# Top-32 attention: eight segments per head in place of nine, ScalarE shifts every column, the selection's product moved between two exchanges

## The chip, the core and the metric

The kernel runs on one core of a Trainium2 chip. The metric is the device time of one execution in microseconds (us). Names of engines: PE is TensorE (PEld its weight loads), DVE is VectorE, ACT is ScalarE, POOL is GpSimd, SP is SyncE, which issues most DMAs.

## What is computed

Attention over 2 batches of 8 heads, 576 tokens of 64 columns, where each query keeps only its 32 highest scores; its output goes to a layer of eight experts, of which each token takes one.

```python
scores = scale * np.matmul(q, k.transpose(0, 1, 3, 2))            # (2, 8, 576, 576)
kth = np.partition(scores, -top_k, axis=-1)[..., -top_k:-top_k + 1]   # top_k = 32
scores = np.where(scores >= kth, scores, -1000000000.0)
attn = np.exp(scores - np.max(scores, axis=-1, keepdims=True))
attn = attn / (np.sum(attn, axis=-1, keepdims=True) + 1e-09)
x = np.matmul(attn, v)                  # reshaped to (1152, 512)
logits = x @ w_gate                     # eight experts; argmax and softmax weight
h = np.maximum(x_e @ w1[e], 0.0)        # per expert e, at most 288 tokens
out = gate_w * (h @ w2[e])
```

The inputs are drawn from a normal distribution. Of each row of 576 scores the 32nd largest is needed exactly.

## The kernel before

**Tiling.** 1152 tokens are 9 tiles of 128, and 8 heads are 4 pairs, so there are 36 units u (`NU`), each 128 queries by two heads (j = 0, 1) by 576 scores. `scores(u)` lets PE write them into PSUM: `s0` (1024 wide, two banks) holds all 576 of head 0 and the first 64 (`TAIL`) of head 1, `s1` holds the other 512 of head 1. Both tiles exist once, so unit u+1 can be written only when all readers of unit u are through.

**The selection of a unit, on DVE.** `heads(u)` runs MAX8 (the eight largest of a row) over segments of each head's row: nine segments of 64 columns, 18 MAX8 (L312). A reduction takes each head's maximum (L315). The first list `nn` holds, negated, the first four or five of each segment (45 columns per head, some of them fillers from `keep`, L316); what is left of each segment's eight is the second list. `merge(u)` takes the eight smallest of the first list (`ns`, L325), removes them by an exchange (MATCH_REPLACE into `wk`, L336, one per head), takes the next eight (`na`, L340) and the eight largest of the second list (`vb`, L339). `bound(u)` makes a lower bound of the 32nd score out of `na` and `vb` (three small instructions, L347, L349, L351).

**The rest of a unit.** ACT's `shift(u)` (L356) reads the scores from PSUM and writes `sm` = maximum minus score into SBUF: 576 columns of head 0, then 512 of head 1; `shift_rest(u)` (L359) does the remaining 64 on DVE. ACT's `sign(u)` (L369) compares `sm` with the bound and counts; POOL's `turn(u)` (L376, two instructions) multiplies `sm` by the signs into `z`; DVE's `select(u)` finds by two MAX8 over 576 columns (L400, steps 1 and 2), a product (`ds`, L402, step 3) and a sum (`nk`, L404, step 4) the exact 32nd score out of the count's excess of 0 to 7. ACT's `penalty` (L413) and PE's and ACT's `probs` (transposes L432 and L433, exponential L434) and PE's `values` (L454, L457) end the unit. Where a count lies outside the range that eight places can mend, `check` sets a flag, and a plain second pass behind the experts computes everything again.

**Order.** The code is a software pipeline written out by hand: step i works on `heads(i)`, `sign`/`turn(i-1)`, `select(i-2)`, `probs(i-3)`, `values(i-4)`, and the scores of i+1. In step i DVE does, in this order, `heads(i)`, `select(i-2)` step 1, the `ns` of `merge(i)`, `shift_rest(i)`, `select(i-2)` step 2, and the rest of `merge(i)`. PE does `values(i-4)`, half of it ahead of `scores(i+1)` and half behind.

**Gaps.** Between two MAX8 of a head `heads` calls `fill()`, which issues one row of a list of small instructions: 8 gaps per head, 16 in a step. The list of a step starts with `bound` (3) and `select` step 0 (L397), then rows of `pick` and `pick_row` in a few steps (they choose the order of experts, from a count that PE's `tally`, L962, has made), three places for `normalise` (L468, L470, L473), and the route of a tile of tokens to its expert (L540 to L563). What does not fit into the gaps runs behind L316.

**Other work beside it.** From step 18 on POOL splits expert weights (L620, L622) in each step's rest; from step 31 on PE also computes the first expert's hidden layer (L661). The experts follow the last unit.

```python
picks = at(2, select, 1) + at(0, merge, None, 0) + at(0, shift_rest) + at(2, select, 2)
run(at(4, values, 0) + picks + at(-1, scores) + at(4, values, 1) + routes((1, 1.5, 3)) + routes((0, 3.5)))
small += at(2, select, 3) + at(2, select, 4)
run(at(0, merge, fill, 1))
```

Here `run(at(0, merge, fill, 1))` issues the rest of `merge`, and the two `fill()` in it issue `select` steps 3 and 4.

Of the kernel before, what the change touches and what calls it, by code (L numbers as in the profile page):

```python
# [19 lines left out]
FT = mybir.dt.float32  # L20
# [5 lines left out]
OP = mybir.AluOpType  # L26
# [3 lines left out]
SEG = 9  # L30
FOUR = 6
# [4 lines left out]
def kernel(  # L36
# [132 lines left out]
    UN = [consts.tile([128, 2, SEG, 9], FT, name=f"un{i}") for i in range(2)]  # L169
    keep = pd[:, 448:448 + 5 * SEG].rearrange("p (s c) -> p s c", s=SEG)  # L170
    nc.vector.memset(keep, -LOW)
    nc.vector.memset(keep[:, :FOUR, 0:1], LOW)
    for un in UN:
        nc.gpsimd.memset(un[:, :, :FOUR, 0:1], LOW)
        nc.gpsimd.memset(un[:, :, FOUR:, 8:9], LOW)
    VB = [pd[:, 32 * i:32 * i + 16].rearrange("p (j c) -> p j c", j=2) for i in range(2)]
# [120 lines left out]
    def segment(u, j, i):  # L297
        w = S // SEG
        if j == 0:
            return PS[u][0][:, i * w:i * w + w]  # L300
        return PS[u][1][:, (i - 1) * w:i * w] if i else PS[u][0][:, S:S + w]


    def heads(u, fill):
        un = UN[u % 2]
# [3 lines left out]
        for j in range(2):  # L309
            for i in range(SEG):  # L310
                o = int(i < FOUR)
                nc.vector.max(out=un[:, j, i, o:o + 8], in_=segment(u, j, i))  # L312
                if i < SEG - 1:
                    fill()
        nc.vector.tensor_reduce(out=mx[:, 0], in_=un[:, :, :, 0:2], axis=mybir.AxisListType.XY, op=OP.max)  # L315
        nc.vector.scalar_tensor_tensor(nn, un[:, :, :, 0:5], -1.0, keep[:, None].to_broadcast([128, 2, SEG, 5]),  # L316
                                       op0=OP.mult, op1=OP.min)
        VAL[u] = [mx, un, nn.rearrange("p j s c -> p j (s c)")]

    def merge(u, fill, half=None):  # L320
# [16 lines left out]
        fill()  # L337
        for j in range(2):
            nc.vector.max(out=vb[:, j], in_=un[:, j, :, 5:])  # L339
# [4 lines left out]
    def bound(u, step):  # L344
        mx, na, vb, tm = VAL[u]
        if step == 0:
            nc.vector.scalar_tensor_tensor(tm, na, -1.0, vb, op0=OP.mult, op1=OP.min)  # L347
# [6 lines left out]
    def shift(u):  # L354
        for j, (o, i) in enumerate(((SM[u][:, 0], PS[u][0][:, :S]), (SM[u][:, 1, TAIL:], PS[u][1]))):
            nc.scalar.activation(o, i, AF.Identity, bias=VAL[u][0][:, 0, j:j + 1], scale=-1.0)  # L356

    def shift_rest(u):
        nc.vector.tensor_scalar(SM[u][:, 1, :TAIL], PS[u][0][:, S:S + TAIL], -1.0, VAL[u][0][:, 0, 1:2],  # L359
                                op0=OP.mult, op1=OP.add)  # L360
# [1036 lines left out]
```

## Time and profile before

| what | us |
|---|---|
| three runs, median (lowest, highest) | 380.05 (379.45, 380.07) |
| the profiled execution, its own time | 379.64 |
| its span in the trace | 377.8 |
| steps 0 to 2 (from the reduction of step 0 to that of step 3) | 14.47 to 33.49 |
| steps 3 to 30 | 33.49 to 209.91 |
| steps 31 to 34 | 209.91 to 241.50 |
| rest of the last unit, routing, count of the experts' tokens | 241.50 to 288 |
| experts | 288 to 377.8 |

"Step i" in times means the stretch from the start of L315 for unit i to its start for unit i+1. A timeline row gives an instruction's start and its length; since instructions on one engine overlap at their ends, what an instruction costs its engine is the distance from its start to the next one's start, called pitch below. The idle time in brackets at the end of a row is the engine's wait before it and what ended the wait.

### The profile page before, as it was taken

How to read it: one execution, taken by the hardware profiler on the slowest of the kernel's cores; microseconds unless marked ns; L12 is line 12 of the kernel's file. 1: busy time of each engine (PE TensorE's matmuls, PEld its weight loads, DVE VectorE, ACT ScalarE, POOL GpSimd, SP SyncE). 2: the span in 40 equal slices, each digit the busy share in tenths (PEclk: the TensorE clock that was granted, in tenths of full speed). 3: DMA queues.
4: the chain of work that ended last, by engine and by line, in shares of the span. 5: the costliest groups of instructions: out<-in, count | busy, mean ns of one | idle time of the engine just before them, and what ended most of it. 6: DMA issues, size and time to landing. Idle time of an engine off the chain costs nothing. (4 is left out here: it accounts for less than half of the span.)

```text
span 377.8 us, 9896 instructions
## 1 busy us (share of the span) xinstructions
PE 318.9 (84%) x3383; PEld 264.7 (70%) x3383; DVE 321.4 (85%) x1708; ACT 278.5 (74%) x464; POOL 240.0 (64%) x280
## 2 busy tenths in 40 slices
PE   5676887798797888987878798999889999999990
PEld 3453666686676766776667687889635999997680
DVE  4879999999999999999999998777665769799930
ACT  5787988888888889898898597774336847786710
POOL 3976969598895598998988886994310101219321
PEclk9778999999999999999999899999999999999997
DMA  9529997948283920000301900832949999999100
GB/s 164 135 57 202 221 208 202 210 120 125 45 272 95 363 75 3 30 2 30 112 2 47 324 22 30 245 120 78 371 97 307 394 304 302 411 302 251 56 24 23
DMA packets 69922, 60.25 MB, mean 159 GB/s; under 512 B 52069, under 2 KB 52069, under 8 KB 69863
## 3 DMA queue, kind: packets, MB, share of 16 engines
q1 hardware_dynamic: 67719, 54.79, 52.9%
q0 software_dynamic: 1616, 4.73, 3.7%
q8 instruction: 28, 0.46, 0.5%
q14 instruction: 31, 0.25, 0.2%
q10 hardware_dynamic: 528, 0.02, 0.1%
HBM read 40.66 MB, written 12.09 MB: 140 GB/s over the span
## 5 line engine op out<-in xcount | busy, mean ns | idle before, releaser
L312 DVE MAX8 un<-s 128x8 f32<-128x64 f32 x648 | 107.0, 217 | 1.0 <-PE s L294 1.0
L376 POOL TENSOR_TENSOR z<-sm,sg 128x576 f32<-128x576 f32 x71 | 90.0, 1286 | 17.7 <-ACT sg L369 17.4
L457 PEld LDWEIGHTS pV<-vm,pT 128*128 128x128 f32 (+1 forms) x640 | 72.3, 183 | 6.9 <-issue 3.6
L681 POOL DMA_INDIRECT out_dram<-y,xp x12 | 24.4, 2032 | 79.8 <-DVE y L857 40.2
L457 PE MATMUL pV<-vm,pT 128*128 128x65 f32 (+1 forms) x640 | 73.2, 262 | 0.0
L413 ACT ACTIVATE pen<-sm,nk 128x576 bf16<-128x576 f32 x71 | 51.4, 768 | 20.6 <-DVE nk L404 20.5
L622 DVE TENSOR_TENSOR ws<-wr,ws 128x1024 bf16<-128x1024 f32 x52 | 61.9, 1238 | 3.3 <-ACT ws L616 2.9
L294 PE MATMUL s<-qk 128*128 128x512 f16 (+3 forms) x320 | 44.0, 297 | 16.8 <-DVE sm L359 16.8
L432 PE MATMUL p<-ident,sm 128*128 128x128 f32 x252 | 50.0, 286 | 7.3 <-ACT xT L526 7.2
L369 ACT ACTIVATE sg<-sm,mx 128x576 bf16<-128x576 f32 x72 | 54.8, 762 | 1.3 <-DVE mx L351 1.3
L400 DVE MAX8 z<-z 128x8 f32<-128x576 f32 x72 | 54.0, 752 | 1.3 <-POOL z L376 1.3
L356 ACT ACTIVATE sm<-s,mx 128x576 f32<-128x576 f32 x72 | 47.5, 711 | 9.7 <-DVE mx L315 9.0
L616 ACT ACTIVATE ws<-wr 128x2048 f16<-128x2048 f32 (+1 forms) x26 | 47.6, 1842 | 6.8 <-issue 4.4
L433 PE MATMUL p<-identB,pen 128*128 128x128 bf16 x252 | 46.0, 223 | 7.7 <-ACT pen L413 7.7
L661 PEld LDWEIGHTS <-ws 128*128 128x128 f16 (+1 forms) x768 | 49.0, 98 | 0.9 <-issue 0.4
L432 PEld LDWEIGHTS p<-ident,sm 128*128 128x128 f32 x252 | 37.0, 147 | 12.0 <-ACT xT L526 8.6
L433 PEld LDWEIGHTS <-pen 128*128 128x128 bf16 x324 | 33.9, 106 | 11.7 <-ACT pen L413 10.8
L294 PEld LDWEIGHTS <-qk 128*128 128x128 f16 (+1 forms) x320 | 20.2, 107 | 28.8 <-issue 20.8
L434 ACT ACTIVATE pT<-p 128x1152 f32<-128x1152 f32 x28 | 31.7, 1132 | 0.0
L622 POOL TENSOR_TENSOR ws<-wr,ws 128x1024 bf16<-128x1024 f32 x12 | 25.6, 2133 | 0.0
L454 PE MATMUL pV<-vt,pT 128*128 128x130 f32 (+1 forms) x80 | 18.1, 308 | 6.1 <-DVE r L540 2.9
L563 POOL DMA_INDIRECT xbuf<-xs,ru x9 | 10.5, 1166 | 17.2 <-DVE un L312 8.1
(277 smaller groups left out, 646.0 us busy)
## 6 DMA issues: line engine op xcount, KB each, us to landing
wr<-in_moe_w_dram SPq DMA_DIRECT2D x32, 1024.0 KB, 8.0
xbuf<-zero SPq DMA_DIRECT2D x6, 771.0 KB, 5.7
qnat<-in_q_dram SPq DMA_DIRECT2D x16, 144.0 KB, 3.4
knat<-in_k_dram SPq DMA_DIRECT2D x16, 144.0 KB, 3.7
out_dram<-zero SPq DMA_DIRECT2D x3, 768.0 KB, 4.7
vm<-in_v_dram SPq DMA_DIRECT2D x16, 128.0 KB, 3.1
qk<-qk SPq DMA_DIRECT2D x14, 144.0 KB, 2.4
vt<-in_v_dram SPq DMA_DIRECT2D x4, 64.0 KB, 4.6
```

The lines of the kernel that those rows point to most:

```text
L294: nc.tensor.matmul(PS[u][a][row:row + n, o:o + w], QK[b][2 * i][:, h, s:s + n], QK[b][1][:, h, c:c + w], start=(i == 0), stop=(i == 1))
L312: nc.vector.max(out=un[:, j, i, o:o + 8], in_=segment(u, j, i))
L369: nc.scalar.activation(SG[u][j], SM[u][:, j], AF.Sign, bias=VAL[u][0][:, 2, j:j + 1], scale=-(1.0 - 2.0 ** -20), accum_out=CNT[:, c:c + 1])
L376: engs[j].tensor_tensor(out=Z[u][:, j], in0=SM[u][:, j], in1=SG[u][j], op=OP.mult)
L400: nc.vector.max(out=z8[:, step - 1], in_=Z[u][:, step - 1])
L413: eng.activation(o, x, AF.Relu, bias=n)
L432: nc.tensor.matmul(pt[:, i], sm[:, cs], ident, start=True, stop=False, is_transpose=True)
L433: nc.tensor.matmul(pt[:, i], pen[:, cs], identB, start=False, stop=True)
L457: nc.tensor.matmul(PV[t][row:row + n, h0 + half], PT[u][:, 5 * half + c, row:row + n], VM[b][:, c, p, half], start=False, stop=(half == 1 ...
L616: nc.scalar.activation(w[:, 0, s], r[:, s], AF.Copy)
L622: eng.tensor_tensor(out=w[:, 1].bitcast(BF)[:, s], in0=r[:, s], in1=w[:, 0, s], op=OP.subtract)
L661: nc.tensor.matmul(o, a(i), c(i), start=(i == 0 and m == 0), stop=(i == k - 1 and m == 2))
```

## The change

- Eight segments per head: 8 of 72 columns for head 0; for head 1 the 64 columns in `s0` and seven pieces of `s1` (six of 73, one of 74). 16 MAX8 per unit over the same 1152 columns.
- The first list takes five of each of eight segments, 40 columns and no fillers; the second list has three of each, 24. `nn` becomes a plain product with a column of -1; `un` comes from the rotating pool `att`; `vb` gets a ninth column in front, which is infinite.
- `shift_rest` is gone; ACT's `shift` has three instructions: 576 columns, 64 columns, 512 columns.
- `select` step 2 is issued right behind step 1, ahead of `ns`; the first `fill()` in the second part of `merge`, which issues `select` step 3 (the product `ds`), moves from behind the two exchanges to between them.

```diff
--- before.py
+++ after.py
@@ -27,8 +27,7 @@
 BIG = float(2.0 ** 90)
 LOW = -3.0e38
 TOPK = 32
-SEG = 9
-FOUR = 6
+SEG = 8
 SPLIT = 256.0
 
 
@@ -166,14 +165,11 @@
 
 
     pd = psum.tile([128, 512], FT, name="pD", bufs=1)
-    UN = [consts.tile([128, 2, SEG, 9], FT, name=f"un{i}") for i in range(2)]
-    keep = pd[:, 448:448 + 5 * SEG].rearrange("p (s c) -> p s c", s=SEG)
-    nc.vector.memset(keep, -LOW)
-    nc.vector.memset(keep[:, :FOUR, 0:1], LOW)
-    for un in UN:
-        nc.gpsimd.memset(un[:, :, :FOUR, 0:1], LOW)
-        nc.gpsimd.memset(un[:, :, FOUR:, 8:9], LOW)
-    VB = [pd[:, 32 * i:32 * i + 16].rearrange("p (j c) -> p j c", j=2) for i in range(2)]
+    minus = pd[:, 448:449]
+    nc.vector.memset(minus, -1.0)
+    VB = [pd[:, 32 * i:32 * i + 18].rearrange("p (j c) -> p j c", j=2) for i in range(2)]
+    for vb in VB:
+        nc.vector.memset(vb[:, :, 0:1], -LOW)
     DM = [pd[:, 64 + 16 * i:80 + 16 * i].rearrange("p (j c) -> p j c", j=2) for i in range(2)]
     M1 = [pd[:, 96 + 2 * i:98 + 2 * i] for i in range(2)]
     tab = pd[:, 104:112]
@@ -295,26 +291,26 @@
                                      QK[b][1][:, h, c:c + w], start=(i == 0), stop=(i == 1))
 
     def segment(u, j, i):
-        w = S // SEG
         if j == 0:
+            w = S // SEG
             return PS[u][0][:, i * w:i * w + w]
-        return PS[u][1][:, (i - 1) * w:i * w] if i else PS[u][0][:, S:S + w]
+        w = 512 // (SEG - 1)
+        return PS[u][1][:, (i - 1) * w:i * w if i < SEG - 1 else 512] if i else PS[u][0][:, S:S + TAIL]
 
 
     def heads(u, fill):
-        un = UN[u % 2]
+        un = att([128, 2, SEG, 8], FT, name="un")
         nn = att([128, 2, SEG, 5], FT, name="nn")
         SM[u] = att([128, 2, S], FT, name="sm", tag="sm", bufs=4)
         mx = att([128, 4, 2], FT, name="mx4", bufs=3)
         for j in range(2):
             for i in range(SEG):
-                o = int(i < FOUR)
-                nc.vector.max(out=un[:, j, i, o:o + 8], in_=segment(u, j, i))
+                nc.vector.max(out=un[:, j, i], in_=segment(u, j, i))
                 if i < SEG - 1:
                     fill()
-        nc.vector.tensor_reduce(out=mx[:, 0], in_=un[:, :, :, 0:2], axis=mybir.AxisListType.XY, op=OP.max)
-        nc.vector.scalar_tensor_tensor(nn, un[:, :, :, 0:5], -1.0, keep[:, None].to_broadcast([128, 2, SEG, 5]),
-                                       op0=OP.mult, op1=OP.min)
+        nc.vector.tensor_reduce(out=mx[:, 0], in_=un[:, :, :, 0], axis=mybir.AxisListType.X, op=OP.max)
+        nc.vector.tensor_tensor(out=nn.rearrange("p j s c -> p (j s) c"), in0=un[:, :, :, 0:5].rearrange("p j s c -> p (j s) c"),
+                                in1=minus[:, None, :].to_broadcast([128, 2 * SEG, 5]), op=OP.mult)
         VAL[u] = [mx, un, nn.rearrange("p j s c -> p j (s c)")]
 
     def merge(u, fill, half=None):
@@ -334,9 +330,10 @@
         vb = VB[u % 2]
         for j in range(2):
             nc.vector.match_replace(out=wk[:, j], in_to_replace=ns[:, j], in_values=nn[:, j], imm_value=LOW)
-        fill()
+            if j == 0:
+                fill()
         for j in range(2):
-            nc.vector.max(out=vb[:, j], in_=un[:, j, :, 5:])
+            nc.vector.max(out=vb[:, j, 1:9], in_=un[:, j, :, 5:])
             nc.vector.max(out=na[:, j], in_=wk[:, j])
         fill()
         VAL[u] = [mx, na, vb, tm]
@@ -344,7 +341,7 @@
     def bound(u, step):
         mx, na, vb, tm = VAL[u]
         if step == 0:
-            nc.vector.scalar_tensor_tensor(tm, na, -1.0, vb, op0=OP.mult, op1=OP.min)
+            nc.vector.scalar_tensor_tensor(tm, na, -1.0, vb[:, :, 0:8], op0=OP.mult, op1=OP.min)
         elif step == 1:
             nc.vector.tensor_reduce(out=M1[u % 2], in_=tm, axis=mybir.AxisListType.X, op=OP.max)
         else:
@@ -352,12 +349,9 @@
 
 
     def shift(u):
-        for j, (o, i) in enumerate(((SM[u][:, 0], PS[u][0][:, :S]), (SM[u][:, 1, TAIL:], PS[u][1]))):
-            nc.scalar.activation(o, i, AF.Identity, bias=VAL[u][0][:, 0, j:j + 1], scale=-1.0)
-
-    def shift_rest(u):
-        nc.vector.tensor_scalar(SM[u][:, 1, :TAIL], PS[u][0][:, S:S + TAIL], -1.0, VAL[u][0][:, 0, 1:2],
-                                op0=OP.mult, op1=OP.add)
+        x, y = PS[u]
+        for j, o, i in ((0, slice(0, S), x[:, :S]), (1, slice(0, TAIL), x[:, S:S + TAIL]), (1, slice(TAIL, S), y)):
+            nc.scalar.activation(SM[u][:, j, o], i, AF.Identity, bias=VAL[u][0][:, 0, j:j + 1], scale=-1.0)
 
     SEL, SG = {}, {}
 
@@ -1092,7 +1086,7 @@
             last = i == NU - 2
             exps = at(3, probs, 0, 1, 2)
             run(exps + at(0, shift) if last else at(0, shift) + exps)
-            picks = at(2, select, 1) + at(0, merge, None, 0) + at(0, shift_rest) + at(2, select, 2)
+            picks = at(2, select, 1) + at(2, select, 2) + at(0, merge, None, 0)
             run(at(4, values, 0) + picks + at(-1, scores) + at(4, values, 1) + routes((1, 1.5, 3)) + routes((0, 3.5)))
             run(mid.get(i, []))
             small += at(2, select, 3) + at(2, select, 4)
@@ -1142,7 +1136,6 @@
         drop()
         run(side.get(L, []))
         shift(L)
-        shift_rest(L)
         penalty(L - 2, (1,))
         merge(L, fill)
         swap_psum("sc", "bk")
```

The order of DVE in step 23, from the reduction to the first MAX8 of the next unit, first of before, then of the change. `un` are the eight largest of each segment, `s` the scores, `pD` a PSUM tile of small things (among them `vb`).

```order
L315 TENSOR_REDUCE mx_2984<-un_125 128x2
L316 SCALAR_TENSOR_TENSOR nn<-un_125,pD 128x90
L400 MAX z_2992<-z 128x8
L325 MAX ns<-nn 128x8 x2
L359 TENSOR_SCALAR sm<-s_2942,mx_2984 128x64
L400 MAX z_2992<-z 128x8
L336 MATCH_REPLACE wk<-ns,nn 128x45 x2
L402 SCALAR_TENSOR_TENSOR ds<-pD,z_2992 128x16
L339 MAX pD<-un_125 128x8
L340 MAX na<-wk 128x8
```

```order
L311 TENSOR_REDUCE mx_2957<-un 128x2
L312 TENSOR_TENSOR nn<-un,pD 128x80
L394 MAX z_2965<-z 128x8 x2
L321 MAX ns<-nn 128x8 x2
L332 MATCH_REPLACE wk<-ns,nn 128x40
L396 SCALAR_TENSOR_TENSOR ds<-pD,z_2965 128x16
L332 MATCH_REPLACE wk<-ns,nn 128x40
L336 MAX pD<-un 128x8
L337 MAX na<-wk 128x8
```

The second selection MAX8 no longer lies between `ns` and the exchange that reads it, and the product lies between the exchanges instead of right ahead of the `vb` MAX8.

DVE again, at the end of `heads(27)`, where `pick` rows fill the gaps; `r` and `ru` are rows of the route. Before, then the change.

```order
L540 COPY r_3300<-pV 128x8
L312 MAX un_125<-s_3411 128x8
L542 MAX r_3301<-r_3300 128x8
L312 MAX un_125<-s_3411 128x8
L315 TENSOR_REDUCE mx_3449<-un_125 128x2
L316 SCALAR_TENSOR_TENSOR nn<-un_125,pD 128x90
L544 MAX_INDEX ru<-r_3301,r_3300 128x8
```

```order
L308 MAX un<-s_3379 128x8 x4
L311 TENSOR_REDUCE mx_3418<-un 128x2
L312 TENSOR_TENSOR nn<-un,pD 128x80
L534 COPY r_3269<-pV 128x8
L536 MAX r_3270<-r_3269 128x8
L538 MAX_INDEX ru<-r_3270,r_3269 128x8
```

With 14 gaps in place of 16, two rows of the route have moved from between MAX8 to behind the reduction.

ACT in one step, before and in the change: shift, exponential, penalty, sign.

```order
L356 ACTIVATE sm<-s_3757,mx_3802 128x576
L356 ACTIVATE sm<-s_3758,mx_3802 128x512
L434 ACTIVATE pT<-p_3860 128x1152
L413 ACTIVATE pen<-sm,nk 128x576 x2
L369 ACTIVATE sg,CNT<-sm,mx_3802 128x576 x2
```

```order
L354 ACTIVATE sm<-s_2432,mx_2479 128x576
L354 ACTIVATE sm<-s_2432,mx_2479 128x64
L354 ACTIVATE sm<-s_2433,mx_2479 128x512
L428 ACTIVATE pT<-p_2523 128x1152
L407 ACTIVATE pen<-sm,nk 128x576 x2
L363 ACTIVATE sg,CNT<-sm,mx_2479 128x576 x2
```

The 64 columns stand between the two others, ahead of the exponential.

## Rows read from the trace of the kernel before

**Rows 1.** The page, part 2: DVE's busy tenths in 40 slices

```profile
DVE  4879999999999999999999998777665769799930
```

**Rows 2.** Busy time by stretch: PE, PEld, DVE, ACT, POOL; PEclk, DMA share, GB/s

```profile
33.49:209.91 176.42, 145.45 (x1410) 120.42 (x1407) 173.91 (x1196) 152.92 (x270) 148.01 (x162) 1.00 0.49 123
209.91:241.50 31.59, 29.18 (x306) 26.00 (x306) 28.93 (x193) 24.86 (x55) 26.42 (x34) 0.95 0.40 123
...
126.44:195.65 69.21, 59.50 (x614) 48.90 (x612) 68.16 (x473) 60.13 (x108) 63.95 (x71) 1.00 0.18 62
210.00:220.00 10.00, 9.41 (x85) 8.14 (x86) 9.27 (x58) 7.74 (x16) 9.02 (x11) 0.83 0.78 286
```

**Rows 3.** Waits, 40 to 225 us: total us, times, longest

```profile
PE s L294 <- DVE sm L359: 13.8, 21, 0.9
```

**Rows 4.** Timeline of DVE in step 23: start, length, what [idle before]

```profile
157.45 0.19 DVE L315 TENSOR_REDUCE mx<-un 128x2 f32<-128x36 f32 x1
...
157.71 0.76 DVE L400 MAX8 z<-z 128x8 f32<-128x576 f32 x1
158.38 0.30 DVE L325 MAX8 ns<-nn 128x8 f32<-128x45 f32 x2
158.60 0.27 DVE L359 TENSOR_SCALAR sm<-s,mx 128x64 f32<-128x64 f32 x1
158.78 0.75 DVE L400 MAX8 z<-z 128x8 f32<-128x576 f32 x1
...
159.79 0.17 DVE L402 SCALAR_TENSOR_TENSOR ds<-pD,z 128x16 f32<-128x16 f32 x1
159.99 0.21 DVE L339 MAX8 pD<-un 128x8 f32<-128x36 f32 x1
...
160.52 0.22 DVE L312 MAX8 un<-s 128x8 f32<-128x64 f32 x1
```

**Rows 5.** Timeline of DVE in `heads(23)`: nine MAX8 without a gap

```profile
155.21 1.27 DVE L312 MAX8 un<-s 128x8 f32<-128x64 f32 x9
156.39 0.15 DVE L540 COPY r<-pV 128x8 f32<-128x8 f32 x1
```

**Rows 6.** Timeline of DVE in step 0, where no product stands

```profile
15.98 0.19 DVE L336 MATCH_REPLACE8 wk<-ns,nn 128x45 f32<-128x45 f32 x1
16.09 0.20 DVE L339 MAX8 pD<-un 128x8 f32<-128x36 f32 x1
```

**Rows 7.** Timeline of ACT in step 22, and 128 columns in the last unit

```profile
151.53 1.32 ACT L356 ACTIVATE sm<-s,mx 128x576 f32<-128x576 f32 x2
152.74 1.13 ACT L434 ACTIVATE pT<-p 128x1152 f32<-128x1152 f32 x1
154.49 1.44 ACT L413 ACTIVATE pen<-sm,nk 128x576 bf16<-128x576 f32 x2 [0.62 <-DVE nk L404]
...
246.12 0.27 ACT L434 ACTIVATE pT<-pV 128x128 f32<-128x128 f32 x1
246.28 0.78 ACT L369 ACTIVATE sg<-sm,mx 128x576 bf16<-128x576 f32 x1
```

**Rows 8.** Timeline of PE: the scores that step 23 issues

```profile
159.00 1.15 PE L294 MATMUL s<-qk 128*128 128x512 f16 x8
```

**Rows 9.** Timeline of DVE in `heads(27)`: a row of `pick` waits for PE

```profile
180.59 0.16 DVE L967 SCALAR_TENSOR_TENSOR pD<-pV,last 1x8 f32<-1x8 f32 x1 [0.30 <-PE pV L962]
```

**Rows 10.** Timeline of POOL (z of unit 22) and of DVE (selection that reads it)

```profile
159.77 2.52 POOL L376 TENSOR_TENSOR z<-sm,sg 128x576 f32<-128x576 f32 x2
...
165.14 0.75 DVE L400 MAX8 z<-z 128x8 f32<-128x576 f32 x1
```

**Rows 11.** Timeline of DVE in step 2

```profile
28.75 0.28 DVE L359 TENSOR_SCALAR sm<-s,mx 128x64 f32<-128x64 f32 x1 [2.18 <-ACT sm L356]
```

**Rows 12.** Timeline of PE: waits in steps 31 and 34

```profile
210.39 0.49 PE L454 MATMUL pV<-vt,pT 128*128 128x130 f32 x2 [2.25 <-DVE r L540]
...
231.89 0.49 PE L454 MATMUL pV<-vt,pT 128*128 128x130 f32 x2 [1.04 <-DVE xr L473]
```

## The prediction

> **What bounds the kernel now.** First the page's slices: DVE is busy nine tenths or more from about 30 to 260 us [rows 1], and the busy times by stretch say how closely: in steps 3 to 30, 28 steps in 176.42 us (6.30 each), DVE works 173.91 us, ACT 152.92, POOL 148.01, PE 145.45 [rows 2]. So here DVE sets the pace, and whatever leaves DVE shortens the step until another engine takes over. Second, the waits: PE stood 13.8 us in all ahead of the scores for DVE's shift of 64 columns, L359 [rows 3]; this is a wait of an engine with time to spare. In steps 31 to 34 it is different: of 31.59 us PE works 29.18 and DVE 28.93, at a mean clock share of 0.95 [rows 2]; both are nearly full, and a gain on DVE alone is not passed on. Behind step 34 the end is a chain over ACT, PE and the loads that begins when the last unit is selected; nothing in it has a fixed date, so it moves as a block.
>
> **The change, DVE part by part, for a step in the middle.**
>
> Segments. Nine MAX8 of 64 columns in a row take 156.39 - 155.21 = 1.18 us, 0.131 each [rows 5]; one of 576 columns has a pitch of 158.38 - 157.71 = 0.67 [rows 4]. Between them lie 512 columns and 0.54 us, 1.05 ns per column; the rest, 0.131 - 0.067 = 0.064 us, is paid per instruction. The 16 new ones read the same 1152 columns, so two instructions are saved: 0.13 us.
>
> The shift of 64 columns. L359's pitch is 158.78 - 158.60 = 0.18 [rows 4]: 0.18 saved.
>
> The product. From `ds` to the next MAX8 (`vb`) 159.99 - 159.79 = 0.20 pass [rows 4], though 16 columns should cost some 0.08 (0.064 + 16 x 1.05 ns); in step 0, which has no product, `vb` follows the exchange after 0.11 [rows 6]. So `vb` waits until the product, 0.17 long, has ended. With the second exchange (0.11) between them that wait is covered: 0.12 saved.
>
> Shorter lists. L315 reads 16 columns instead of 36, L316 80 for 90, two each of L325, L336 and L340 40 for 45, two L339 24 for 36: 84 columns less at 1.05 ns, 0.09.
>
> The added wait. The exchange used to run a whole selection MAX8 after `ns` and now follows it at once. Two `ns` are 0.30 long in all with a pitch of 0.11 [rows 4], so the first is finished 0.19 after its start, and the exchange could start at 0.21: nearly nothing, 0.02. If it waits for both, 0.10. Queued behind it are the rest of `merge` and the next unit's MAX8.
>
> Sum per step 0.13 + 0.18 + 0.12 + 0.09 - 0.02 = **0.50 us**. Bounds: 0.36 if the product's stall stays and the wait is 0.04; 0.55 if a MAX8 between small rows costs a little more than in a row.
>
> **What must keep up.** ACT gets a third shift instruction, which the trace lacks. ACT's two shifts have a pitch of 1.21 together, 0.605 for 544 columns on average, and one of 128 columns 246.28 - 246.12 = 0.16 [rows 7]: drawn on to 64 columns this is 0.09; the 128-column row is 0.27 long, an upper end. I take 0.20, towards the upper end, since the shift reads a bias per row as the 1152-column exponential in [rows 7] doesn't. In the step it lies ahead of the exponential; ACT now waits 0.62 after it for `nk` [rows 7], which covers it. The Trainium skill ("ScalarE: Activation LUTs", section "What ACT_TABLE_LOAD costs") gives about 280 ns plus 0.833 ns per column with such a bias, of which some 93 ns overlap with a neighbour; worked out as an estimate, 0.24 for 64 columns. By 0.24 in place of 0.20, ACT would need 1.1 us more in 28 steps, and the first rival below would be a little likelier; its 0.64 for 544 columns is a little over the trace's 0.605.
>
> PE may start the scores of the next unit when ACT has read `s0`: the shift starts some 0.25 after the reduction (which is 0.19 long), then 0.64 and 0.20 and 0.1 until the wait is seen, 1.2 us. It needs 0.65 for the part in `s0` (56% of 1.15 [rows 8]); DVE's first MAX8 of the next unit comes 160.52 - 157.45 - 0.37 = 2.70 after it (the heads keep 0.13 of the 0.50) [rows 4]. That leaves 0.8. In step 23, in which a tile lies across the two batches, PE is late by its own work: scores start 159.00 - 157.45 = 1.55 after the reduction [rows 8], and PE doesn't get faster while DVE does; I count a stall of 0.24 once.
>
> POOL's `z` of unit 22 ends at 162.29, and the selection's second MAX8 reads it at 165.14 [rows 10]: 2.85 us in hand. In the change this MAX8 comes 0.4 earlier in its step, and eight steps later DVE is 4 us ahead; but POOL itself now loses time waiting for DVE. I count nothing here and leave the rest to a rival.
>
> **What the steps do not give.** In `heads(27)` a row of `pick` waits 0.30 for PE's tally [rows 9], and one in `heads(31)` does the same; PE's time for it is set by PE's own queue, so DVE's gain ahead of it turns into waiting. Steps 26 and 30 give about nothing: -1.0. With 14 gaps for 16, small rows that depend on each other drain behind L316, each at its length and a gap, about 0.2 (L540 is 0.15 long [rows 5]), instead of the 0.07 that it adds between two MAX8: one in `heads(17)`, two more in `heads(27)`: -0.43. With step 23's 0.24 steps 3 to 30 give 28 x 0.50 - 1.0 - 0.43 - 0.24 = **12.3**.
>
> Steps 0 to 2 are paced by waits. In step 2 L359 waits 2.18 for ACT's shift [rows 11], and `select` step 2 and all of `merge` stand behind it. Without it DVE is ready early and waits for PE's scores, which need only ACT's reading. I count 0.25 in steps 0 and 1 (scores begin some 0.13 sooner, heads 0.13 shorter) and 0.9 in step 2: **1.4**.
>
> In steps 31 to 34 PE starts when DVE's row of the route is done (2.25 of waiting), works on, and waits again 1.04 in step 34 for DVE's `xr` [rows 12]. `xr` moves behind the reduction too (14 gaps), 0.2 later, and a tally waits for PE once more. I count +0.2 here, and -0.3 in the last unit, where ACT's third shift lies in ACT's own chain: **-0.1**.
>
> Sum: 12.3 + 1.4 - 0.1 = 13.6. The profiled execution took 379.64, of which 377.8 is the span: 366.0. The median of the runs is 0.41 above that execution: **366.4**.
>
> **The rivals.**
>
> ACT takes over. Its 152.92 in 28 steps are 5.46 each; with 0.20 it is 5.66, against 5.86 of the new step, 97%. It has a loop of its own, `nk`, penalty, sign, next shift, in which it still waits for DVE. If 0.15 of idle time per step stays beside 0.27 for the new instruction, the step is 5.88 plus what the copies of xT make uneven, say 6.0: the 28 steps give 8.4, and the time is 370.3. For it: the small reserve. Against it: a late ACT delays `z` and the scores, which have 2.85 and 0.8 in hand. Chance 0.12.
>
> POOL takes over where it splits weights. From step 18 to 28 it is busy 63.95 of 69.21 us [rows 2]; the new eleven steps would take about 64.7. If its gaps stay as they are, bar the one wait for DVE, it needs 68.0: 3.3 lost, 369.7. Against: POOL starts with a reserve of about 3 us, which lasts nearly to the end. Chance 0.13.
>
> Only the counted instructions pay: the stall of the product moves elsewhere, and 0.36 is left: 28 x 0.14 = 3.9 less, 370.3. Chance 0.13.
>
> More comes: 0.55 per step (1.4), and the granted clock of step 31, 0.83 from 210 to 220 [rows 2] behind PE's wait of 2.25 [rows 12], stays full: PE's 9.41 us there would shrink by up to 1.6, of which I count 1: 364.0, and less if the tallies are early. Chance 0.14.
>
> Slower: the second pass. The new bound holds only if no row has too many of its 32 in the lower ranks of its segments. A row whose count lies 8 or more above 32 sets the flag, and everything is computed again. That pass alone has, per unit, 8 MAX8 and 6 exchanges of 576 columns at some 0.67 [rows 4], 9.4 us, 338 us in 36 units: over 700 in all. From the drawn inputs I worked out the counts under both bounds: the largest excess is 7 in both, in three of the 9216 rows before and in one with the new segments, though rows with any excess grow from 607 to 867. One row at 8 would decide it. Chance 0.02, with 0.01 for other ways to be slower.
>
> **How the numbers follow.** The forecast of 366.4 has 0.43, with its own range 364.5 to 368.5. ACT 0.12, POOL 0.13, small gain 0.13, more 0.14, slower 0.03, within 0.2% (which is about what a measurement of this kernel can tell from no change) 0.02. The range goes from 362.0, all steps at 0.55 with none of the tally waits and a full clock, to 371.5, which holds the three rivals with a small gain and some of two at once. Faster 0.95, same 0.02, slower 0.03.
>
> **What would show it.** In the trace after: pitch of the pair of selection MAX8 unchanged, `vb` about 0.1 behind the second exchange, reduction to first MAX8 of the next unit 2.70 instead of 3.07, ordinary steps near 5.45 to 5.9; steps 26 and 30 as long as before with longer waits for the tally; no DVE wait for POOL's `z`. Wrong would be DVE waits ahead of the segments or of L400 in each step (then ACT, PE or POOL sets the pace), or MAX8 of 72 columns at much over 0.14.

## The result

| | before | after |
|---|---|---|
| median (lowest, highest), us | 379.75 (378.28, 380.07) | 368.53 (367.86, 369.43) |
| ratio, 95% interval | | 0.9714 (0.9680 to 0.9747) |
| span of the profiled execution | 377.8 | 366.1 |
| to the reduction of step 0 | 14.47 | 13.53 |
| steps 0 to 2 | 19.02 | 17.70 |
| steps 3 to 30 | 176.42 | 167.62 |
| steps 31 to 34 | 31.59 | 32.32 |
| behind step 34 | 136.30 | 134.93 |

The change gained 11.2 us, where 13.6 was forecast. Of the first stage and the last it touches one unit each, and how long they take goes by the execution more than by the kernel: over all profiled executions of this study the first lay between 13.3 and 14.5 us, also among kernels with the same first stage, and the last between 134.7 and 136.3. So the 2.3 us that the two profiled executions differ by there are taken for luck. In the steps themselves the change gained 1.3 + 8.8 - 0.7 = 9.4.

The answers to [rows 2], busy time by stretch in the kernel after (PE, PEld, DVE, ACT, POOL, then PEclk, DMA share, GB/s):

```profile
31.23:198.85 167.62, 145.20 (x1403) 120.68 (x1402) 163.69 (x1113) 156.59 (x296) 147.50 (x162) 0.99 0.49 130
198.85:231.17 32.32, 30.34 (x305) 27.12 (x305) 27.48 (x182) 25.52 (x59) 26.46 (x34) 0.90 0.37 122
```

DVE has 10.2 us less work in steps 3 to 30, and is now idle for 3.9 us of them where it was for 2.5. ACT has 3.7 more. In steps 31 to 34 DVE's work fell too, and yet they are longer, at a lower clock.

DVE in step 25, the answer to [rows 4] (start, length, what):

```profile
159.21 0.18 DVE L311 TENSOR_REDUCE mx<-un 128x2 f32<-128x16 f32 x1
...
159.45 1.41 DVE L394 MAX8 z<-z 128x8 f32<-128x576 f32 x2
160.78 0.28 DVE L321 MAX8 ns<-nn 128x8 f32<-128x40 f32 x2
161.00 0.09 DVE L332 MATCH_VALUE_LOAD wk<-ns,nn 128x8 f32 x1
...
161.18 0.17 DVE L396 SCALAR_TENSOR_TENSOR ds<-pD,z 128x16 f32<-128x16 f32 x1
161.26 0.08 DVE L332 MATCH_VALUE_LOAD wk<-ns,nn 128x8 f32 x1
161.33 0.18 DVE L332 MATCH_REPLACE8 wk<-ns,nn 128x40 f32<-128x40 f32 x1
161.43 0.18 DVE L336 MAX8 pD<-un 128x8 f32<-128x24 f32 x1
...
161.95 0.24 DVE L308 MAX8 un<-s 128x8 f32<-128x72 f32 x1
```

`vb` (L336) starts 0.10 behind the second exchange, as forecast: the product `ds` no longer stands in front of it. The exchange's first instruction starts 0.22 behind the pair of `ns`, whose pitch is 0.11 each: next to no wait. From the reduction to the next unit's first MAX8, in most steps, 2.71 us pass (in this step 161.95 - 159.21 = 2.74); 3.07 did before and 2.70 was forecast.

The waits that are new or larger, from the list of all waits between 13 and 232 us (engine, line, what for: us in total, times, longest):

```profile
PE s L290 <- ACT sm L354: 11.1, 15, 1.9
...
DVE un L308 <- PE s L290: 5.5, 8, 1.9
...
ACT sg L363 <- POOL z L370: 4.9, 8, 1.7
...
PE pV L448 <- DVE r L534: 3.8, 2, 2.7
...
DVE pD L961 <- PE pV L956: 1.5, 2, 1.1
DVE pD L984 <- PE pV L956: 1.3, 2, 0.7
```

The third of these isn't in the trace of before at all, and is the way by which 1.4 us of the missing gain went, as the experiments show. POOL's own waits say the same from the other side: from 13 us to the last unit's reduction it waited 17.4 us for ACT's `sg` in the kernel before, and 6.1 in this one.

### The profile page after: what moved, and what is told of

Read it like the earlier page. It is cut to its first block, busy times and chain, and to the rows that moved or that the text cites. A ratio compares the mean times of both kernels' runs of the same rounds, so it can differ in the third digit from the quotient of the medians.

```text
span 366.1 us, 9855 instructions
## 1 busy us (share of the span) xinstructions
PE 317.0 (87%) x3380; PEld 264.4 (72%) x3383; DVE 306.6 (84%) x1601; ACT 284.2 (78%) x500; POOL 240.9 (66%) x276
## 5 line engine op out<-in xcount | busy, mean ns | idle before, releaser
L308 DVE MAX8 un<-s 128x8 f32<-128x72 f32 (+2 forms) x576 | 102.1, 224 | 5.7 <-PE s L290 5.5
L451 PEld LDWEIGHTS pV<-vm,pT 128*128 128x128 f32 (+1 forms) x640 | 73.3, 185 | 6.9 <-issue 3.6
L451 PE MATMUL pV<-vm,pT 128*128 128x65 f32 (+1 forms) x640 | 74.2, 264 | 0.0
L354 ACT ACTIVATE sm<-s,mx 128x576 f32<-128x576 f32 (+2 forms) x108 | 54.8, 582 | 7.6 <-DVE mx L311 7.5
L394 DVE MAX8 z<-z 128x8 f32<-128x576 f32 x72 | 51.0, 748 | 1.2 <-POOL z L370 1.1
L655 PEld LDWEIGHTS <-ws 128*128 128x128 f16 (+1 forms) x768 | 49.2, 99 | 0.9 <-issue 0.4
L290 PEld LDWEIGHTS <-qk 128*128 128x128 f16 (+1 forms) x320 | 20.0, 106 | 22.4 <-issue 14.1
L836 PEld LDWEIGHTS <-ws 128*128 128x128 f16 (+1 forms) x288 | 21.3, 98 | 0.0
```

What stands on the lines that cost most here:

```text
L290: nc.tensor.matmul(PS[u][a][row:row + n, o:o + w], QK[b][2 * i][:, h, s:s + n], QK[b][1][:, h, c:c + w], start=(i == 0), stop=(i == 1))
L308: nc.vector.max(out=un[:, j, i], in_=segment(u, j, i))
L354: nc.scalar.activation(SM[u][:, j, o], i, AF.Identity, bias=VAL[u][0][:, 0, j:j + 1], scale=-1.0)
L451: nc.tensor.matmul(PV[t][row:row + n, h0 + half], PT[u][:, 5 * half + c, row:row + n], VM[b][:, c, p, half], start=False, stop=(half == 1 ...
L655: nc.tensor.matmul(o, a(i), c(i), start=(i == 0 and m == 0), stop=(i == k - 1 and m == 2))
```

## Each part alone

Three kernels take the kernel before and make one part of the change.

**The product.**

> The kernel before with one edit: the product of the selection is issued between the two exchanges instead of behind both. My term says the first small MAX8 (vb) no longer waits for the product's end: ds to vb still about 0.3 with the exchange between, vb about 0.10 behind the second exchange where it was 0.20 behind the product, 0.12 us per step in steps 3 to 30. In these 28 steps 3.0 to 3.4 less, and 376.3 to 377.0 us in all. Rival (the stall only moves to another place): the 28 steps as long as before and 379.4 to 380.2.

```diff
             nc.vector.match_replace(out=wk[:, j], ...)
-        fill()
+            if j == 0:
+                fill()
```

**The shift.**

> The kernel before with one edit: ScalarE shifts all 1152 columns in three instructions and VectorE's shift of 64 columns is gone. My term: 0.18 us per step in steps 3 to 30 less what the tally waits take back, 4 to 5 us there, and 0.9 to 1.1 in step 2, whose wait of 2.18 ends: 373.5 to 375. ScalarE's three shifts 1.41 from the first's start to the exponential instead of 1.21. Rival (ScalarE, with 0.20 more, or GpSimd holds the step up): under 2.5 us in the 28 steps, 376.5 or more, with waits of VectorE ahead of the first MAX8 of a unit in many steps.

The edit is the new `shift` of the change, without `shift_rest`, and nothing else.

**The segments.**

> The kernel before with the eight segments, their shorter lists and the memsets that go with them; VectorE still shifts 64 columns, and the product stands behind both exchanges. My terms: 0.13 for two MAX8 and 0.09 for 84 columns, 0.22 per step; from the trace of the changed kernel, in which the 16 MAX8 with what stands in their gaps saved 0.09 and not 0.13, 0.18 per step. In steps 3 to 30 4.5 to 6 less without the waits for the tally, 3.5 to 5 with them: 374.5 to 376. Rival (two gaps fewer: small rows drain at their full length, which eats the two MAX8): 0.09 per step and less than 2.5 in all, 377.5 or more.

The edit is the changed kernel with `shift_rest`, the order of `picks` and the place of `fill()` put back.

Measured: product 375.12, ratio 0.9896 (0.9866 to 0.9926); shift 373.35, 0.9849 (0.9793 to 0.9905); segments 373.46, 0.9855 (0.9798 to 0.9913). All three times lie below what was expected. Of the profiled executions' gains 1.2, 1.3 and 2.8 us lie outside the steps, as above, so the parts are read from the steps (us, from one reduction's start in the timeline to the next):

| step | before | product | shift | segments | after |
|---|---|---|---|---|---|
| 5 | 6.36 | 6.22 | 6.22 | 6.12 | 5.89 |
| 6 | 5.86 | 5.75 | 5.74 | 5.66 | 5.42 |
| 19 | 6.35 | 6.22 | 6.22 | 6.12 | 5.90 |
| 4 | 5.86 | 5.97 | 5.73 | 5.66 | 5.85 |
| 16 | 6.66 | 6.54 | 6.53 | 6.36 | 6.84 |
| 24 | 5.95 | 5.83 | 5.83 | 5.74 | 5.78 |
| 26 | 7.05 | 7.05 | 6.99 | 6.87 | 7.38 |
| 30 | 7.85 | 7.86 | 7.86 | 7.89 | 8.37 |
| 3 to 30 | 176.42 | 173.31 | 173.00 | 171.02 | 167.62 |

In an ordinary step the product gives 0.13 (0.12 forecast), the segments 0.20 to 0.24 (0.22), the shift 0.13 (0.18). Together 0.48, and the changed kernel has 0.45. In 28 steps the three parts alone gave 3.1, 3.4 and 5.4 (the shift less than the 4 to 5 that I expected of it, the segments more than 3.5 to 5), together 11.9; the whole change gave 8.8. So it is not that a part doesn't pay: 3.1 us are lost only in the whole change. Of these 2.2 lie in five steps of the table: 0.73 in step 16, 0.57 in 26, 0.46 in 30, 0.28 in 24 and 0.21 in 4. The rest is 0.04 in each of the others, most of it the changed order of the selection's MAX8, which none of the three parts has (0.03, measured below). Steps 26 and 30 give a single part little or nothing, as forecast. Step 4 is no clear case: with the product alone it was longer too.

The shift's missing 0.05 is at one row. Up to the first MAX8 of the next unit step 23 gained 0.19 with it (3.07 to 2.88, all of the shift's 0.18), but then the counts' row of `select` (L397 of before) lies 0.19 behind its MAX8 instead of 0.14. So it is, at 0.18 to 0.20, in all kernels that have ACT's third instruction, and at 0.14 to 0.16 in the three that don't. Why is open.

**The order of the selection's MAX8.**

> The changed kernel with the second MAX8 of the selection put back behind the two ns, as in the kernel before, so that the exchange doesn't follow ns at once. My term for the added wait is 0.02 per step, bound 0.10: by 0.02 this kernel runs 0.6 us less to 0.3 more than the changed one, 367.8 to 368.9, by 0.10 it is 2.5 to 3 us faster, 365.5. The trace of the changed kernel shows the first exchange 0.1 behind the second ns, so I expect the former. A third result, slower by 0.5 to 1.5: the selection ends 0.6 later for nk and dm, and ScalarE, which now waits for the sign's buffer, loses more.

```diff
-            picks = at(2, select, 1) + at(2, select, 2) + at(0, merge, None, 0)
+            picks = at(2, select, 1) + at(0, merge, None, 0) + at(2, select, 2)
```

Measured: 368.96, 0.9732 (0.9673 to 0.9792), the same as the changed kernel. In ordinary steps it is 0.03 shorter (5.39 for 5.42, 5.86 for 5.89), so the added wait is 0.03 where 0.02 was put down. But its step 12 took 6.55 instead of 5.52 and its step 16 7.29. In both, ACT had waited for POOL's `z` (0.91 and 0.37 ahead of step 12's shift, 0.88 and 0.37 ahead of step 16's): the wait of the list above, in step 12 where the changed kernel has none.

## Where the missing 3 us went: POOL holds ACT, ACT holds PE, PE holds DVE

Step 16 of the changed kernel (reduction at 105.68), ACT, PE, POOL and DVE:

```profile
104.83 0.78 ACT L363 ACTIVATE sg<-sm,mx 128x576 bf16<-128x576 f32 x1 [0.77 <-POOL z L370]
...
106.06 0.78 ACT L363 ACTIVATE sg<-sm,mx 128x576 bf16<-128x576 f32 x1 [0.37 <-POOL z L370]
...
106.84 1.50 ACT L354 ACTIVATE sm<-s,mx 128x576 f32<-128x576 f32 x3
```

```profile
107.82 1.21 PE L290 MATMUL s<-qk 128*64 128x512 f16 x16 [1.36 <-ACT sm L354]
110.02 0.17 PE L956 MATMUL pV<-OHS,onesb 128*1 128x8 bf16 x1
```

```profile
103.52 4.99 POOL L370 TENSOR_TENSOR z<-sm,sg 128x576 f32<-128x576 f32 x4
```

```profile
110.22 0.16 DVE L961 SCALAR_TENSOR_TENSOR pD<-pV,last 1x8 f32<-1x8 f32 x1 [0.46 <-PE pV L956]
```

POOL is behind: it makes `z` of two units in a row (four instructions). The sign `sg` has two buffers, those of one unit, so ACT can write the next unit's first sign only when POOL has read the last one's. ACT, whose queue is in order, then starts the shift 106.84 - 105.68 = 1.16 after the reduction instead of 0.28. PE waits for that before the scores, the tally stands behind the scores, and a row of `pick` on DVE waits for the tally.

**More buffers for the sign.**

> The changed kernel with four buffers instead of two for the sign (sg), so that ScalarE may write the next unit's sign while GpSimd still reads the last one's. Theory (GpSimd's lateness reaches ScalarE by these buffers, and from there the shift, TensorE's scores and VectorE): ScalarE's waits of 4.9 us for z fall under 0.5, the shift of step 16 comes 0.3 instead of 1.16 behind the reduction, VectorE's waits for the scores and the tallies get 0.5 to 1.5 us smaller, and the time is 367 to 368. Rival (GpSimd itself is the bound there): the wait moves to the MAX8 of the selection, which waits for z, and the time stays at 368.5 or over.

```diff
-            SG[u] = [att([128, S], BF, name="sg") for j in range(2)]
+            SG[u] = [att([128, S], BF, name="sg", bufs=4) for j in range(2)]
```

Measured: 368.71, 0.9718 (0.9643 to 0.9793), no gain in all, where 367 to 368 was expected; but the steps say why. Step 16 went from 6.84 to 6.29, 24 from 5.78 to 5.52, 26 from 7.38 to 6.81: 1.4 us, as the theory has it, with ACT's waits for `z` gone but for one of 1.7 in step 34, which the changed kernel has too. Step 30 grew from 8.37 to 9.16. There the wait for the tally is the old 0.65; another instruction is longer:

```profile
194.08 2.30 DVE L989 TENSOR_TENSOR row<-rows 1x1 int32<-1x1 f32 x1
```

```profile
194.32 2.05 POOL L614 TENSOR_SCALAR ws<-wr 128x1024 f16<-128x1024 f32 x2
```

**One element, 2.30 us.** DVE's sum of two numbers ends at 196.38, and POOL's two conversions of weights end at 196.37. In the changed kernel the same pair reads:

```profile
195.47 1.50 DVE L989 TENSOR_TENSOR row<-rows 1x1 int32<-1x1 f32 x1
```

```profile
194.90 2.06 POOL L614 TENSOR_SCALAR ws<-wr 128x1024 f16<-128x1024 f32 x2
```

195.47 + 1.50 = 196.97, and 194.90 + 2.06 = 196.96. In the kernel before, whose line numbers differ, it was 206.95 + 0.90 = 207.85 against 205.79 + 2.05 = 207.84:

```profile
206.95 0.90 DVE L995 TENSOR_TENSOR row<-rows 1x1 int32<-1x1 f32 x1
```

```profile
205.79 2.05 POOL L620 TENSOR_SCALAR ws<-wr 128x1024 f16<-128x1024 f32 x2
```

DVE's instruction, with two operands from SBUF, is held until POOL has finished, and gets no turn between POOL's two. In the first pair it even began ahead of the conversions, beside POOL's last `z` (until 194.36), and was held through all three. It is not every two-operand instruction beside POOL: L391 of the changed kernel, one of whose operands lies in PSUM, took 0.18 at 194.01, during POOL's `z` (192.41 to 194.93). The Trainium skill ("SBUF — State Buffer", section "SBUF: two separate sides") states this: VectorE with two SBUF inputs and GpSimd reading SBUF share a pair of ports as an exclusive lock, and the later one waits for the whole instruction. The three pairs here agree with that to 0.01 us, and in them the wait passes over the boundary between GpSimd's two instructions.

**The sum in another form.**

> The changed kernel with one instruction in another form: the sum of two columns in pick_row (1 element) is a tensor_scalar with its second operand as a pointer, where a tensor_tensor read two columns of SBUF. In the changed kernel it took 1.50 us in step 30 and ended with GpSimd's conversion of weights. Theory (VectorE's two-operand read is held until that GpSimd instruction ends): it takes 0.18 in both places, step 30 is 7.0 to 7.1 instead of 8.37, and the time is 367.0 to 367.6. Rival (the instruction is long because it waits for its operand, or something else in the step is as late): step 30 stays over 8 and the time at 368.3 to 368.8.

```diff
-            nc.vector.tensor_tensor(out=row[:, e:e + 1], in0=rows[:, e, 0:1], in1=rows[:, e, 1:2], op=OP.add)
+            nc.vector.tensor_scalar(row[:, e:e + 1], rows[:, e, 0:1], rows[:, e, 1:2], None, op0=OP.add)
```

Measured: 365.41, 0.9643 (0.9590 to 0.9695), a larger gain than expected. The sum takes 0.18 though POOL's conversions run beside it:

```profile
197.03 0.18 DVE L989 TENSOR_SCALAR row<-rows 1x1 int32<-1x1 f32 x1
```

```profile
196.47 2.06 POOL L614 TENSOR_SCALAR ws<-wr 128x1024 f16<-128x1024 f32 x2
```

Step 30 is 7.05 instead of 8.37, as expected. And more came behind it: step 31 6.43 (7.86 in the changed kernel), 32 5.51 (6.14), 33 7.17 (7.67). PE in step 31, in the changed kernel and then in this one:

```profile
199.30 0.80 PE L448 MATMUL pV<-vt,pT 128*128 128x130 f32 x2 [2.66 <-DVE r L534]
```

```profile
199.54 0.49 PE L448 MATMUL pV<-vt,pT 128*128 128x130 f32 x2 [1.34 <-DVE r L534]
```

The busy time and clock of step 31 in the two:

```profile
198.85:206.71 7.86, 7.41 (x51) 6.48 (x52) 6.52 (x44) 4.97 (x10) 6.68 (x9) 0.57 1.02 371
```

```profile
199.09:205.52 6.43, 5.72 (x64) 5.04 (x65) 6.33 (x43) 5.74 (x13) 6.23 (x9) 1.00 0.91 308
```

Behind 2.66 us of waiting PE worked at 0.57, most of the step at the lower of its two levels (1.2 GHz), and behind 1.34 at the full 2.4 GHz. The step was 7.28 at 0.77 in the kernel before. So steps 31 to 34, which the change made 0.7 longer, take 29.79 here. One instruction on one element, 1.3 us longer than its work, cost 1.3 in its own step and 2.5 behind it.

The 2.5 is not a fixed price. The kernel with the order put back, above, has the same held sum (step 30 took 8.41) and a slightly longer wait, but a higher clock in step 31:

```profile
200.52 0.57 PE L448 MATMUL pV<-vt,pT 128*128 128x130 f32 x2 [2.71 <-DVE r L534]
```

```profile
200.06:207.00 6.94, 6.48 (x56) 5.58 (x57) 6.39 (x44) 5.17 (x12) 6.25 (x9) 0.75 0.97 364
```

Its steps 31 to 34 took 30.97, so there the sum cost about 1.2 behind its own step. How far the clock falls isn't settled by the length of the wait.

Steps 3 to 30 are no shorter than in the changed kernel for all that (167.93), since this kernel keeps the two buffers: ahead of step 12 ACT waited 1.18 and 0.37 for `z`, PE then 1.76 for ACT, PE's clock fell (0.77 from 82 to 97 us), and the steps 12 and 13 took 6.94 and 7.19 where 5.52 and 5.95 are usual.

The stretch from 82 to 97 us:

```profile
82.00:97.00 15.00, 12.55 (x94) 10.20 (x93) 12.53 (x82) 13.23 (x28) 13.71 (x17) 0.77 0.48 88
```

**Rows of pick and route moved.**

> The changed kernel with small rows moved only: normalise rows that do nothing are dropped from steps with rows of pick, the rows of the route stand right behind those of pick_row in the gaps of the units 31 and 34, and the sum of pick_row is a tensor_scalar. Theory (14 gaps are too few there, so the route's rows drain behind the reduction, and the two-column tensor_tensor of 1.50 us is held up beside GpSimd): steps 30 and 33 lose 1 us each at most, step 31 no longer begins with 2.66 of TensorE's waiting but with 1.5, the granted clock in 200 to 210 us is over 0.8 instead of 0.72: 365 to 367. Rival (TensorE waits there for VectorE's chain as a whole, and where the rows stand doesn't matter): 368 to 369.

The edit, in the step's list of small rows, beside the sum above: `normalise`, which does nothing in odd steps, is left out of an odd step with rows of `pick`, and in the units that have rows of `pick_row` (31 and 34) the route's rows stand right behind those.

```diff
-            small += early.get(i, []) + late.get(i, [])
-            small += at(5, normalise, 0) + at(5, normalise, 1) + at(5, normalise, 2) + routes((2, 2.1, 2.2, 4, 5, 5.5))
+            todo = early.get(i, []) + late.get(i, [])
+            more = at(5, normalise, 0) + at(5, normalise, 1) + at(5, normalise, 2)
+            more = (more if i % 2 == 0 or not todo else []) + routes((2, 2.1, 2.2, 4, 5, 5.5))
+            small += todo[:3] + more + todo[3:] if todo and todo[0][0] is pick_row else todo + more
```

Measured: 365.54, 0.9666 (0.9589 to 0.9743). Against the sum alone: step 27 5.90 (6.43), step 31 6.35 (6.43), and steps 31 to 34 29.29 (29.79). Step 27's 0.5 is the drained row of the forecast: L534 used to run behind the reduction and now has a gap. Step 16 took 7.54, by the wait for `z` again, which this kernel keeps. In all it can't be told from the sum alone.

**Both mends.**

> The changed kernel with the four sg buffers and the moved rows of pick and route, tallies where they were. Theory (the combination that was 369.6 failed by the tallies alone, at which TensorE stood and its clock fell): sg gives 1.4 in the steps 16, 24 and 26, the rows 1.3 in step 30 and 3.0 in steps 31 to 34: steps 3 to 30 in 164.5 to 165.5, 31 to 34 in 29.2 to 29.8, time 361.5 to 363.5. Rival (the buffers and the rows meet on one bound): 365 or more, with step 16 over 7 us.

Measured: 364.48, 0.9636 (0.9598 to 0.9673), short of the 361.5 to 363.5 expected; steps 3 to 30 164.45, as expected, 31 to 34 30.31, 0.5 more than the upper end. ACT in step 16 of this kernel (reduction at 105.69), to be set beside the rows of the changed kernel above:

```profile
103.97 0.76 ACT L363 ACTIVATE sg<-sm,mx 128x576 bf16<-128x576 f32 x1
...
105.96 1.52 ACT L354 ACTIVATE sm<-s,mx 128x576 f32<-128x576 f32 x3 [0.38 <-DVE mx L311]
107.37 1.14 ACT L428 ACTIVATE pT<-p 128x1152 f32<-128x1152 f32 x1
```

ACT waits for DVE again, step 16 is 6.21 and 24 is 5.51; there is no wait for `z` left on ACT in this trace. Steps 3 to 30 give 11.97 against before. Steps 31 to 34 are 1.0 longer than with the rows alone: step 34 takes 11.18 for 10.18, and in it DVE waits 0.92 for POOL's `z`, which it doesn't there. So POOL can still be late, here for DVE in place of ACT. That the buffers bring this about isn't shown: with the tallies moved as well (next section) there is no such wait. The interval of both mends lies below that of the changed kernel (0.9680 to 0.9747), so it beats both kernels, by 3 to 4 us the second; from the sum alone (0.9590 to 0.9695) it can't be told.

## The waits for the tally: two attempts that failed

**Tallies ahead of the scores.**

> The changed kernel with the four tallies put ahead in TensorE's queue, so that they no longer stand behind the scores of their step. Theory: the rows of pick wait for the tally only because it stands behind the scores; their waits of 0.46, 1.06, 0.66 and 0.65 (2.8 us in steps 16, 26, 30 and 33) fall under 0.2 each, and the steps 16, 26 and 30 get 2 us shorter: 366 to 367. Rival (the tally waits for something else, for VectorE's own dm or mask): the waits stay and the time is 368 to 369.

```diff
-    mid[16] = [(tally, 0)]
+    side.setdefault(16, []).append((tally, 0))
```

and so for steps 26, 30 and 33.

Measured: 369.93, 0.9757 (0.9685 to 0.9829): 1 us worse if anything. DVE still waits 0.33, 0.96 and 0.96 in steps 16, 26 and 30, but the profile now puts these waits down to PE's rows of the route, L544 and L523, though the row reads the tally:

```profile
173.05 0.16 DVE L961 SCALAR_TENSOR_TENSOR pD<-pV,last 1x8 f32<-1x8 f32 x1 [0.96 <-PE pV L523]
```

Why a row of `pick` waits for them, with the tally long done, is open.

**With all the mends:**

> The changed kernel with the three mends together: four buffers for sg, tallies ahead of the scores, rows of pick and route moved. Theory (the three losses are separate): their gains add to 3.5 to 6 us, 362.5 to 365. Rival (all three sit on one bound, GpSimd or TensorE, which stays): no better than the best of the three alone, 366 or more.

Measured: 369.60, 0.9739 (0.9646 to 0.9831); the kernel with the same mends but the old tallies had 364.48. The four executions lie between 367.5 and 372.1, and the trace is that of a long one (371.43). PE in step 15 of the kernel with all the mends:

```profile
105.32 0.17 PE L956 MATMUL pV<-OHS,onesb 128*1 128x8 bf16 x1 [1.83 <-DVE xr L467]
```

PE's queue is in order too. The tally now stands at its head, and PE waits 1.83 for DVE with the transposes and the values queued behind. Step 16 then ran at a clock of 0.54 and took 10.19 (6.21 with the old tallies), step 26 9.24 (7.09) and step 30 9.25 (7.10): 8.3 us lost in this execution. In the kernel with the tallies alone the same wait of 1.83 was followed by a clock of 1.00, and step 16 took 6.93. Step 16 in this kernel, then in that one, with its wait:

```profile
105.87:116.06 10.19, 10.19 (x68) 8.09 (x67) 6.31 (x48) 5.77 (x12) 5.23 (x7) 0.54 0.32 116
```

```profile
107.84 0.17 PE L956 MATMUL pV<-OHS,onesb 128*1 128x8 bf16 x1 [1.83 <-DVE xr L467]
```

```profile
108.39:115.32 6.93, 6.19 (x70) 5.12 (x68) 6.21 (x45) 6.42 (x14) 4.04 (x6) 1.00 0.46 170
```

Which of the two comes isn't settled by the length of the wait.

**Rows of the route first.**

> As the run with sg and rows together, but the rows of the route stand ahead of the rows of pick_row and pick in the gaps, so that the first row that needs the tally comes three to four gaps later. Theory (the wait of 0.65 for the tally has a fixed end, and rows that don't need it fit ahead of it): the waits in steps 30 and 33 fall under 0.1, step 30 is 6.5 instead of 7.1, and TensorE gets the route 0.6 sooner; 360.5 to 362.5, 0.5 to 1.3 under the other. Rival (TensorE is the bound in 31 to 34, and VectorE's earlier end is waited away): the same as the other within 0.3.

**And with the order of the selection put back:**

> As the run before it, with the second MAX8 of the selection behind the two ns, as in the kernel of before. Alone this order gave 0.035 per ordinary step, but lost 1.0 in step 12 and 0.45 in step 16, where ScalarE waited for GpSimd's z at the sign's buffer. Theory (those losses go with the two more buffers): 5.39 and 5.86 in ordinary steps, step 12 at 5.5, 0.7 to 1.1 less in steps 3 to 30, and 359.8 to 361.8. Rival (a VectorE that is faster by 1 us only meets GpSimd's loads, which come at fixed times): step 12 or 16 long again, the time as the run before it or over.

Against the kernel with both mends, both have this edit; the second has the line of `picks` from the order above as well:

```diff
-            more = (more if i % 2 == 0 or not todo else []) + routes((2, 2.1, 2.2, 4, 5, 5.5))
-            small += todo[:3] + more + todo[3:] if todo and todo[0][0] is pick_row else todo + more
+            small += (more if i % 2 == 0 or not todo else []) + routes((2, 2.1, 2.2, 4, 5, 5.5)) + todo
```

Measured: 365.76, 0.9668 (0.9603 to 0.9732) and 364.97, 0.9624 (0.9574 to 0.9675); neither can be told from the 364.48 of both mends, and both miss what was expected (360.5 to 362.5 and 359.8 to 361.8). In the first of the two DVE waits as long as before, at the route's row:

```profile
194.71 0.17 DVE L534 COPY r<-pV 128x8 f32<-128x8 f32 x1 [0.65 <-PE pV L956]
```

```profile
193.57 1.01 PE L523 MATMUL pV<-wg,xT 128*128 128x8 f32 x8
194.51 0.17 PE L956 MATMUL pV<-OHS,onesb 128*1 128x8 bf16 x1
```

PE issues the route's product (L523) and the tally one behind the other at the end of its work for the step, so both kinds of row wait for the same end, some 4.4 behind the reduction. My theory, that the route's rows were ready, was wrong. In the second kernel ordinary steps are 5.38 to 5.39 and 5.86 to 5.87, and step 12 is 5.48: with four buffers the order no longer loses there. Each of the two lost elsewhere: the first waited for `z` on DVE in steps 15 and 16 (0.33, then 0.18 and 0.47), which took 6.32 and 7.00, and the second took 6.88 in step 4, with PE at 0.72.

## Why the prediction was right, and where it was off

The time, 368.5, lay in the range, 2.1 above the forecast. Part of that nearness is luck: to the steps the prediction gave 12.3 + 1.4 + 0.2 = 13.9 (and 0.3 less in the last unit), and 9.4 came; the 2.3 of the first stage and the last made up for half of the difference. In steps 3 to 30 it is 8.8 for 12.3. Of the 3.5 that are missing, 1.3 lie in the term of the ordinary step, 1.8 in steps 16, 24, 26 and 30, and 0.4 in step 4; the rest nearly cancels.

- **Terms of an ordinary step.** Right in size: 0.13, 0.22 and 0.13 measured alone for 0.12, 0.22 and 0.18, and 0.03 for the added wait of 0.02. The sum is 0.45 for 0.50, by the shift's 0.05; in the 26 steps that it was counted for 1.3 us of the difference.
- **ACT's third shift.** From the first shift to the exponential 1.41 us pass (105.96 to 107.37 above) where 1.21 did [rows 7]: 0.20, as put down.
- **Steps 26 and 30.** Counted as giving nothing; they became 0.33 and 0.52 longer. The tally's wait was rightly seen as ended by PE's queue; that this queue would itself be late (ACT's shift, step 26) and that a sum would be held beside POOL (step 30) was not. In step 30 of before that sum already took 0.90; I had not asked why.
- **Step 23.** A stall of 0.24 was counted; 0.41 of the 0.45 came. Too cautious.
- **Rows that drain.** 0.43 was counted for steps 17 and 27; they gained 0.08 and 0.40 less than an ordinary step. About right.
- **POOL's reserve.** This is the step that failed, a wait that the sum put at nothing. I took the 2.85 us from `z` to the selection [rows 10] for all that POOL had in hand, and counted nothing, because only DVE's MAX8 was looked at as a reader. The other one who depends on POOL is ACT, by the two buffers of the sign, and there the reserve was gone seven times up to step 26. DVE's own wait for `z` did not appear before the last unit, as forecast. Steps 16, 24 and 26 lost 1.4 us by it, which four buffers gave back.
- **Steps 31 to 34.** A gain of 0.2 was forecast, and they became 0.7 longer. (The forecast's -0.1 holds 0.3 lost in the last unit too, which no run measured apart.) That PE starts there when DVE's row of the route is done was right [rows 12]; that row came later by the held sum, and the clock fell to 0.57 in step 31 from 0.77.
- **Steps 0 to 2.** 1.3 for 1.4, but from other steps: step 0 became 0.5 longer and steps 1 and 2 0.3 and 1.5 shorter, where gains of 0.25, 0.25 and 0.9 were put down. Step 0 took 5.8 to 5.9 in all kernels whose first reduction came at 13.3 to 13.5, and 5.1 to 5.6 in those where it came at 14.1 to 14.5, so it gives back much of a quick start. The agreement is luck in part.
- **Step 4.** It gave nothing (0.45 expected): PE's clock was 0.74 at its start, behind 1.90 of waiting for ACT in step 3. Here too the wait doesn't settle it: behind the same 1.90 step 4 took 5.39 at the full clock with the order put back, and 6.88 in the last kernel above. That the 0.4 is the change's doing isn't shown.
- **The rivals.** The one on POOL splitting weights named the right engine with the wrong path and, for step 16, the wrong place; ACT as the bound did not come, nor did the second pass. The product's stall did not move elsewhere (0.13 alone), and the clock of step 31 fell further where the hopeful rival had it stay full.

## What to carry to other kernels

When the engine that sets the pace is made faster, list for each engine beside it every buffer that it must free, not only who reads its result: with two buffers of one unit, an engine behind by a microsecond stops a third one, and an in-order queue passes that on. And a row that takes ten times its work is worth a question before anything else: set its end beside the ends of the other engines' rows.

## What was not expected of the hardware

- DVE's `tensor_tensor` of one element with two SBUF operands was held 0.90, 1.50 and 2.30 us beside POOL's 1024-column conversions, to their end within 0.01; as `tensor_scalar` with a pointer it took 0.18.
- PE's clock behind a wait: 0.57 in the step that began with 2.66, 0.75 with 2.71, 1.00 with 1.34; behind the same 1.83, 0.54 once and 1.00 once.
